# Batch 4 of eight scores its keys on small tiles of TensorE, and a new set of ranks orders all the work

## The chip, the core and the metric

One core of a Trainium2 chip runs the kernel. Its engines work side by side: TensorE multiplies matrices (PE; its weight loads are PEld), VectorE (DVE) and ScalarE (ACT) work on elements, GpSimd (POOL) and SyncE (SP) mostly issue transfers (DMA). The metric is the time of one execution in microseconds (us), as a median of several runs; lower is better.

## The reference

Two attentions follow each other, then two dense layers. The inputs are float32: `q`, `k`, `v` of 8 batches, 8 heads, 576 tokens and 64 values per head, and `p`, 32 landmark tokens per head.

```python
p_packed = sm_attn(p, k, v)           # 32 landmarks look at 576 keys
out = sm_attn(q, p_packed, p_packed)  # 576 queries look at the 32 packed landmarks
x = out.transpose(0, 2, 1, 3).reshape(B * S, H * D)      # 4608 x 512
h = x @ w_in                                             # 512 -> 2048
g = where(h >= 1, h, where(h <= -1, 0, (h + 1)**2 / 4))  # smelu
return g @ w_out                                         # 2048 -> 512
```

`sm_attn` is softmax attention with scale 1/8. The output is 4608 x 512 float32.

## The kernel before

All the work is cut into some 1,500 steps, batch by batch. One batch goes through these stages, each named by its tile and line:

- `k` and `q` are loaded as bf16 by POOL (L352) and turned so that the head's 64 values lie on partitions: in batches 0 and 1 by TensorE (L471), from batch 2 on by a transposing transfer that SP issues (`crossed`, L500, tiles `kT`, `qT`).
- Scores of the landmarks against the keys. There are two forms. In `scores` (L528) the keys are the weights and the landmarks stream through: 24 matmuls of 128 x 64 into `sp`, keys on partitions, then two exponentials on ACT (L533, tile `ex`). In `turned_scores` (L557) the landmarks are the weights, in tiles of 64 rows by 32 columns, and the keys stream: 16 matmuls of 288 columns into two `s1` tiles, landmarks on partitions; ACT takes two exponentials (L564, tile `exn`), each of which also sums its rows into `ks`. There the exponentials lie the wrong way round for the next product, so `untwisted` (L581) turns `exn` back with a transposing transfer on SP into `exT`. `TURN` (L220) is the first batch that takes the second form.
- The packed landmarks `pk` (L619, 24 matmuls): exponentials times values. The values are first regrouped on DVE (L602, tile `vv`, one buffer). In the first form 12 matmuls more, of two columns each (`key_sums`, L634), give the softmax sums; in the second form they are in `ks` already, and DVE makes `rs` from them in two instructions (L666, L667) and not one (L669).
- `ppT` (copies of `pk`), scores of the queries `s2` (L700), exponentials `eT`, sums by a matmul (`sm`, L728), logarithm and exponential for the reciprocal (`ln`, `rc`), the weights of the second attention `A` on DVE (L742); `mp` (L686) is the packed landmarks times `w_in`, copied to `M`.
- The hidden layer `h` (L814, 16 tiles a batch, 4 matmuls each; it needs both halves of `A`), then the smelu in three steps: `x` on ACT (L820), `t` on ACT or DVE (L830, L828), `hT` on DVE (L835).
- The output `o` (L889, 16 matmuls of 512 columns per block of 128 tokens, 36 blocks), a copy `ob`, and two stores by SP (L908).

What stands in which order on each engine is settled while the program is built, in `Plan.run`. Each step has a rank from a table (`AT`, `HID`, `OUT`, `L1`), the engines it may run on with assumed costs, what it depends on and the buffers it takes; a list scheduler with models of the engines, of the load queue and of SP's transfers then picks the ready step of the lowest rank, and the instructions are emitted in that order. On the chip every engine works through its list strictly in order and waits on semaphores, so a step whose input is late holds up all that stands behind it on its engine. `o` matmuls are the material with which the planner fills TensorE while a chain on other engines runs.

Buffers matter for the transfers: one for `k`, one for `v`, one for `vv`, two each for `q`, `kT`, `qT`; three tiles `w` of PSUM are shared by all stages but the output. The load of a batch's `k` waits for the transposing transfer of the batch before to have landed, that of `v` for both `vv` copies of the batch before. All loads stand in one queue on POOL, all transposing transfers and nearly all stores on SP.

Of the kernel before, what the change touches and what calls it, by code (L numbers as in the profile page):

```python
# [183 lines left out]
def kernel(  # L184
# [32 lines left out]
    MB0 = {("k", 0, 4): 0.75, ("v", 0, 0): 1.35, ("q", 0, 0): 0.5}  # L217
    MB1 = {("w_in", 0, 0): 0.7, ("w_in", 0, 1): 0.7}
    FIRST = 2
    TURN = 5  # L220
    PAIRED = 2
    MERGED = 2
    SPLIT, AHALF, WPARTS, MPARTS, QLATE, ORDER3, ORDER = 2, 1, 1, 0, 1, 0, 2
    Q0 = [range(0, 8, 2), range(1, 5, 2), range(5, 9, 2)]
    LOADS = "k0 v0 q0 win0 win1 wout0 k1 win2 win3 wout1 v1 wout2 q1 wout3 v2 q2 p k2"
    LENT = [1, 3, 4]
    L1 = 15.967
    AT = [dict(kT=148.161, qT=275.48, sc=149.063, pk=-49.085, s2=-3.905, sm=-182.602, M=178.569, **{"M+": -129.863}),
          dict(kT=-39.644, qT=-48.123, sc=-66.351, pk=124.743, s2=170.079, sm=-187.478, M=-105.149, **{"M+": 146.812}),
          dict(kT=115.732, qT=51.477, sc=130.42, pk=237.931, s2=-181.084, sm=-29.758, M=169.369, **{"M+": -44.412}),  # L230
          dict(kT=29.446, qT=-25.092, sc=52.472, pk=243.839, s2=179.754, sm=-32.11, M=115.586, **{"M+": -71.343}),
          dict(kT=38.536, qT=86.402, sc=153.04, pk=258.796, s2=-13.152, sm=-43.327, M=-95.344, **{"M+": 110.184}),
          dict(kT=1.864, qT=113.754, sc=282.551, pk=400.409, s2=-26.009, sm=-92.874, M=125.845, **{"M+": 0.958}),
          dict(kT=126.633, qT=239.492, sc=-4.526, pk=382.024, s2=-90.437, sm=32.434, M=177.14, **{"M+": -62.453}),
          dict(kT=27.261, qT=148.76, sc=40.741, pk=216.362, s2=-45.985, sm=130.271, M=1.019, **{"M+": -201.613})]
    HID = [(27.4, 1.3921), (-10.054, 2.601), (22.49, 3.9747), (126.895, 4.8485), (231.121, 9.6612), (-18.141, 4.6461), (3.622, 15.8949), (451.41, 5.8147)]
    OUT = [[(235.954, -183.0), (268.544, -106.533), (35.947, 20.528), (122.624, -48.891)],
# [7 lines left out]

    V, A_, G_ = nc.vector, nc.scalar, nc.gpsimd
    nc.scalar.preload_act_table_set("natural_log_exp_and_others")
# [203 lines left out]
    def attention(b, at, fine):  # L451
# [63 lines left out]
        def scores(i, pairs):  # L515
            n, h0, last = len(pairs), G * pairs[0], (G * pairs[-1] + G) * E - 1

            def mm(e):
                have["sp", b, i] = sp = wide([P, 4 * X * G, n * NP], f32, "sp")
                kT = have["kT", b].rearrange("p h e t -> p (h e t)")  # L520
                for c in range(E):
                    for g in range(G):
                        for k, a in enumerate(pairs):

                            j = (G * a + g) * E + c
                            w = TP if j == last else P
                            o = sp[:w].rearrange("p (c x g) (a n) -> p c x g a n", x=X, g=G, a=n)[:, c, :, g, k]
                            nc.tensor.matmul(o, kT[:, j * TP:j * TP + w], pT[:, b, g, a], start=True, stop=True)  # L528

            def ex(e):  # L530
                if i == 0:
                    have["ex", b] = new("ex", [TP, E * X * G, Q * NP], bf16)
                nc.scalar.activation(have["ex", b][:, :, NP * pairs[0]:NP * (pairs[-1] + 1)],  # L533
                                     have["sp", b, i][:TP, :E * X * G], AF.Exp, scale=scale)

            r = at["sc"] + 0.25 * n * i
            t = plan.add(r, {"PE": (0.03 + 0.18 * n, 0.2 + 0.18 * n, mm)}, ready["k", h0] + pT_of[b],
                         ["w", "ex"] if i == 0 else ["w"])
            x = plan.add(r + 0.01, {"ACT": (0.1 + 0.32 * n, 0.16 + 0.32 * n, ex)}, [t], behind=exs[-1:])
            exs.append(x)  # L540
            plan.release("w", [x])
            return t

        exs = []
        if b == 0:
            pads.append(plan.add(-27, {"DVE": (0.8, 0.8, lambda e: [V.memset(exn[..., TP:], 0.0), V.memset(
                pT[:, 2:TURN].rearrange("p b g a x n -> p (b g a x n)"), 0.0)])},
                                 [consts], behind=ready["k", 4]))

        def turned_scores():  # L550
            def mm(e):
                for g in range(G):
                    have["s1", b, g] = s1 = wide([P, X, FW], f32, "s1")
                    for a in range(Q):
                        for x in range(X):
                            r = slice(x * D, (x + 1) * D)
                            nc.tensor.matmul(s1[a * NP:(a + 1) * NP, x, :HALF], pT[r, b, g, a, x],  # L557
                                             have["kT", b][r, G * a + g].rearrange("p e t -> p (e t)"),
                                             start=True, stop=True)

            def ex(e, g):
                if g == 0:
                    have["ks", b] = new("ks", [P, G], f32)
                nc.scalar.activation(exn[:, g, :, :, :TP],  # L564
                                     have["s1", b, g][:, :, :HALF].rearrange("p x (e t) -> p x e t", e=E),
                                     AF.Exp, scale=scale, accum_out=have["ks", b][:, g:g + 1])

            t = plan.add(at["sc"], {"PE": (0.28, 0.43, mm)}, ready["k", 0] + pT_of[b], ["w"] * G, mode="s")
            before = None
            for g in range(G):  # L570
                ready[f"ex{g}"] = before = plan.add(
                    at["sc"] + 0.2 * g + 0.01, {"ACT": (0.8, 0.87, lambda e, g=g: ex(e, g))}, [t],
                    ["exn", "ks"] if g == 0 else [], behind=[before])
                plan.release("w", [before])
            return t
# [11 lines left out]

        turned_k = b >= TURN
        plan.release("kT", [turned_scores()] if turned_k else [scores(i, ps) for i, ps in enumerate([[0], [1], [2], [3]] if b == 0 else [[0, 1], [2, 3]])])
# [323 lines left out]
    for b in range(B):  # L913
        if b == 2:
            landmarks(2, B, L1, [landed["p"], identity])
        attention(b, AT[b], b == 0)
        for fi in range(KF):
            hidden(b, fi, HID[b][0] + HID[b][1] * fi)
        plan.release("M", h_of[b])
        plan.release("A", h_of[b])  # L920
        first = 0 if b % 2 == 0 else 4
        for j, (start, span) in enumerate(OUT[b]):
            widths = (256, 128, 128) if (b, first + j) == (B - 1, 8) else (d_model,)
# [54 lines left out]
```

## Time and profile before

| | before |
|---|---|
| median of 3 runs | 243.35 us (242.96 to 243.61) |
| profiled execution, its own time | 242.94 us |
| its span, first to last instruction | 241.1 us |
| PE busy | 233.3 us (97%) |
| ACT busy | 192.7 us (80%) |
| DVE busy | 177.6 us (74%) |
| POOL busy | 31.4 us (13%) |
| granted TensorE clock | 1.00 in nearly every stretch |

The profile counts an engine as busy while an instruction is on it. The matmuls of PE overlap in the pipeline, so one of 512 columns is shown with some 379 ns, while the next starts 216 ns after it; what a matmul costs is the distance of the starts, and that is how its rows are read here. The views used are the page with its chain of waits, the busy time by stretches, the instructions in order of time of single engines, the groups by form, and the answers on one line of the program, which tell who waited and how long a transfer took from issue to landing.

### The profile page before, as it was taken

What the parts mean: (1) busy time and instruction counts of PE and PEld (TensorE: products, weight loads), DVE (VectorE), ACT (ScalarE), POOL (GpSimd) and SP (SyncE); (2) the same over time, 40 slices, a digit from 0 to 9 for tenths busy, and PEclk for the clock granted to TensorE, in tenths of its full rate; (3) what the DMA queues carried; (4) which work ended last, traced back from release to release, by engine and by line L of the source; (5) the groups of instructions that cost most, each with busy time, mean ns of one, the idle gap of its engine ahead of it and who ended that gap; (6) DMA issues with size and microseconds to landing.
All of it is one profiled execution on the core that took longest, in us unless ns stands there. A gap on an engine that the chain in (4) does not pass through costs nothing.

```text
span 241.1 us, 5370 instructions
## 1 busy us (share of the span) xinstructions
PE 233.3 (97%) x2117; PEld 133.9 (56%) x2154; DVE 177.6 (74%) x311; ACT 192.7 (80%) x342; POOL 31.4 (13%) x47
## 2 busy tenths in 40 slices
PE   8999999999999999999999999999999999999995
PEld 2646555466554665466645564465546644565454
DVE  4549997678967998789936898689999955899000
ACT  3779996988969985999776988999789988888111
POOL 8462006200220040030030003000000000000000
PEclk9999999999999999999999999999999999999999
DMA  7999999996999999999999999999930301202233
GB/s 158 196 206 207 206 205 205 197 241 132 125 198 149 234 164 251 152 221 221 194 165 246 233 141 147 161 141 226 191 94 4 85 5 44 71 21 65 65 87 90
DMA packets 64138, 37.03 MB, mean 154 GB/s; under 512 B 36720, under 2 KB 59632, under 8 KB 64112
## 3 DMA queue, kind: packets, MB, share of 16 engines
q0 software_dynamic: 24336, 18.25, 52.6%
q1 hardware_dynamic: 38960, 17.87, 36.7%
q10 hardware_dynamic: 816, 0.56, 0.8%
q8 instruction: 17, 0.28, 0.5%
q14 instruction: 9, 0.07, 0.1%
HBM read 37.22 MB, written 9.44 MB: 194 GB/s over the span
## 4 chain that ended last, share of the span: by engine, by line
PE 81%; DVE 6%; DMA 5%; ACT 4%; POOL 2%; issue 2%; POOLq 0%; ACTq 0%
PE o L889 48%; PE h L814 21%; DMA w_in_sb<-in_moe_w_in_dram 5%; DVE hT L835 4%; PE mp L686 3%; PE pk L619 2%; PE sm L728 1%; DVE t L828 1%; ACT x L820 1%; PE sp L528 1%; PE s L700 1%; ACT t L830 1%; POOL q L352 1%; ACT M L271 1%; PE o L942 1%
## 5 line engine op out<-in xcount | busy, mean ns | idle before, releaser
L889 PE MATMUL o<-w_out_sb,hT 128*128 128x512 bf16 (+2 forms) x574 | 140.9, 367 | 1.9 <-issue 0.6
L835 DVE SCALAR_TENSOR_TENSOR hT<-t 128x576 bf16<-128x576 f32 (+1 forms) x130 | 93.7, 746 | 4.3 <-ACT t L830 2.3
L820 ACT ACTIVATE x<-h 128x576 f32<-128x576 f32 (+1 forms) x130 | 78.6, 651 | 9.1 <-PE h L814 8.5
L889 PEld LDWEIGHTS <-hT 128*128 128x128 bf16 x608 | 55.8, 98 | 49.8 <-issue 6.1
L814 PE MATMUL h<-A,M 128*128 128x288 bf16 x512 | 78.5, 286 | 0.6 <-ACT M L271 0.3
L814 PEld LDWEIGHTS <-M 128*128 128x128 bf16 x512 | 49.9, 98 | 27.6 <-issue 1.1
L830 ACT ACTIVATE t<-x 128x576 f32<-128x576 f32 (+1 forms) x57 | 39.4, 693 | 0.6
L828 DVE TENSOR_SCALAR t<-x 128x576 f32<-128x576 f32 (+1 forms) x73 | 33.3, 456 | 7.1 <-ACT x L820 6.7
L271 ACT COPY ob<-o 128x512 f32<-128x512 f32 (+2 forms) x22 | 12.0, 552 | 17.0 <-PE o L889 16.9
L742 DVE SCALAR_TENSOR_TENSOR A<-eT,rs,rc 128x576 bf16<-128x576 bf16 (+1 forms) x18 | 12.8, 748 | 11.5 <-ACT rc L737 11.5
L271 ACT CAST M<-mp 128x1024 bf16<-128x1024 f32 (+1 forms) x20 | 19.1, 992 | 2.7 <-PE mp L686 2.7
L352 POOL DMA_DIRECT2D k<-in_k_dram x8 | 6.7, 843 | 87.8 <-DMA kT<-k 68.4
L271 DVE CAST M<-mp 128x1024 bf16<-128x1024 f32 (+1 forms) x13 | 15.3, 1180 | 3.1 <-PE mp L686 3.1
L271 DVE COPY ob<-o 128x512 f32<-128x512 f32 x16 | 10.8, 688 | 6.9 <-PE o L889 6.9
L723 ACT ACTIVATE eT<-s,rs 128x576 bf16<-128x576 f32 x16 | 11.1, 742 | 2.5 <-PE s L700 2.5
L942 PE MATMUL o<-zeros 128*128 128x512 bf16 (+1 forms) x35 | 10.5, 431 | 1.3 <-DVE zeros L307 1.2
L732 ACT ACTIVATE ln<-sm 128x576 f32<-128x576 f32 x16 | 10.3, 652 | 1.2 <-PE sm L728 0.7
L686 PE MATMUL mp<-w_in_sb,ppT 64*32 64x512 bf16 x256 | 10.9, 380 | 0.2
L271 ACT CAST ppT<-pk 64x128 bf16<-64x128 f32 x24 | 6.2, 260 | 5.7 <-PE pk L634 4.0
L737 ACT ACTIVATE rc<-ln 128x576 f32<-128x576 f32 (+1 forms) x18 | 10.4, 625 | 0.1
L352 POOL DMA_DIRECT2D v<-in_v_dram x8 | 6.2, 779 | 21.9 <-PE pk L624 15.2
L533 ACT ACTIVATE ex<-sp 96x768 bf16<-96x768 f32 (+1 forms) x12 | 8.1, 709 | 0.5 <-PE sp L528 0.4
(59 smaller groups left out, 116.7 us busy)
## 6 DMA issues: line engine op xcount, KB each, us to landing
v<-in_v_dram POOLq DMA_DIRECT2D x8, 576.0 KB, 11.6
out_dram<-ob SPq DMA_DIRECT2D x23, 192.0 KB, 4.5
k<-in_k_dram POOLq DMA_DIRECT2D x7, 576.0 KB, 8.7
q<-in_q_dram POOLq DMA_DIRECT2D x7, 576.0 KB, 12.8
out_dram<-ob SPq DMA_DIRECT2D x24, 128.0 KB, 2.9
w_out_sb<-in_moe_w_out_dram POOLq DMA_DIRECT2D x4, 512.0 KB, 19.7
w_in_sb<-in_moe_w_in_dram POOLq DMA_DIRECT2D x3, 512.0 KB, 15.2
out_dram<-ob SPq DMA_DIRECT2D x23, 64.0 KB, 4.5
```

What stands on the lines that cost most here:

```text
L271: i = (nc.vector.tensor_copy if e == "DVE" else nc.scalar.copy)(to, of)
L352: G_.dma_start(tokens(nm, b)[:, heads(hs)], rows_of(nm, b, hs))
L686: m = nc.tensor.matmul(have["mp", b, f][a * NP:(a + 1) * NP, g], have["ppT", b][r, g, a], w_in_sb[r, a, f * FW:(f + 1) * FW], start=True, ...
L723: nc.scalar.activation(have["eT", b, g], have["s2", b, g][:, :, :HALF], AF.Exp, scale=rs_of[b][:, g, 1:])
L742: V.scalar_tensor_tensor(have["A", b][:, g, xs], have["eT", b, g][:, xs], rs_of[b][:, g, :1], have["rc", b, g][:, xs], ALU.mult, ALU.mult)
L814: nc.tensor.matmul(have["h", b, fi][:, hf, :HALF], have["M", b][:, g, fi * P:(fi + 1) * P], have["A", b][:, g, hf], start=(g == 0), stop=( ...
L820: nc.scalar.activation(have["x", b, fi][:, hs[0]:hs[-1] + 1], have["h", b, fi][:, hs[0]:hs[-1] + 1, :HALF], AF.Prelu, bias=-1.0, alpha=0.5)
L828: V.tensor_scalar(t, x, 1.0, 0.0, ALU.add, ALU.max)
L830: nc.scalar.activation(t, x, AF.Relu, bias=1.0)
L835: V.scalar_tensor_tensor(dst, t, 1.0, t, ALU.min, ALU.mult)
L889: nc.tensor.matmul(have["o", key][:, :w], hT[:, fi, i * P:(i + 1) * P], w_out_sb[:, fi, cols], start=(fi == 0), stop=(fi == KF - 1))
L942: nc.tensor.matmul(o[:, :w], zeros[:, :P], zeros[:, :w], start=True, stop=True)
```

## The change

`TURN` goes from 5 to 4, so batch 4 takes the second form (`turned_scores` and `untwisted`) in place of the first. All numbers of `L1`, `AT`, `HID` and `OUT` are new, so the planner orders all steps anew. No other line differs. Two lines of the table stand for all of it.

```diff
-    TURN = 5
+    TURN = 4
...
-    L1 = 15.967
-    AT = [dict(kT=148.161, qT=275.48, sc=149.063, pk=-49.085, s2=-3.905, sm=-182.602, M=178.569, **{"M+": -129.863}),
...
+    L1 = 24.006
+    AT = [dict(kT=-40.556, qT=-2.912, sc=90.446, pk=28.864, s2=-33.904, sm=-3.662, M=340.906, **{"M+": -180.41}),
```

With it the pad that is zeroed at the start (L546, `pT` of batches 2 to TURN - 1) shrinks from 768 to 512 elements.

What moves, at two places. First SP in the stretch of batch 4's packed landmarks: the turned keys `kT` and queries `qT` of batch 5 (L500), the stores of finished blocks (L908), and the exponentials that are turned back (L581). Before, with nothing to turn back for batch 4; the L581 at the end is batch 5's:

```order
L908 DMA out_0_dram<-ob_1796 96x512
L500 DMA_TRANSPOSE kT_1884<-k_1767 128x24x96
L500 DMA_TRANSPOSE qT_1985<-q_1547 128x24x96
L908 DMA out_0_dram<-ob_2043 64x512 x2
L908 DMA out_0_dram<-ob_2115 96x512
L908 DMA out_0_dram<-ob_2115 32x512
L908 DMA out_0_dram<-ob_2128 32x512
L908 DMA out_0_dram<-ob_2128 96x512
L908 DMA out_0_dram<-ob_2209 64x512 x2
L908 DMA out_0_dram<-ob_2266 64x512 x2
L581 DMA_TRANSPOSE ex_2336<-exn_81 128x12x128
```

The same place on SP now; the L581 here is batch 4's:

```order
L908 DMA out_0_dram<-ob_1735 32x512
L908 DMA out_0_dram<-ob_1801 64x512 x2
L581 DMA_TRANSPOSE ex_1938<-exn_81 128x12x128
L908 DMA out_0_dram<-ob_1985 96x512
L908 DMA out_0_dram<-ob_1985 32x512
L500 DMA_TRANSPOSE kT_2012<-k_1712 128x24x96
L500 DMA_TRANSPOSE qT_2034<-q_1518 128x24x96
L908 DMA out_0_dram<-ob_2037 64x512 x2
```

The transfer that turns batch 4's exponentials back, and the store of one block, now stand ahead of batch 5's `kT` and `qT`.

Second DVE around the weights `A` of batch 2 (L742). The two L602 rows are the regrouping of batch 3's values, which needs the load of batch 3's `v`. Before:

```order
L271 CAST ppT_1214<-pk_1216 64x128 x2
L669 RECIPROCAL rs_1215<-pk_1216 128x4
L271 CAST M_1284<-mp_1285 128x2x512
L271 COPY ob_1307<-o_1000 128x512
L742 SCALAR_TENSOR_TENSOR A_1353<-eT_1295,rs_1215,rc_1321 128x576
L742 SCALAR_TENSOR_TENSOR A_1353<-eT_1301,rs_1215,rc_1351 128x576
L271 CAST M_1284<-mp_1342 128x2x512
L602 COPY vv_1384<-v_1212 96x4x6x64 x2
L835 SCALAR_TENSOR_TENSOR hT_80<-t_1393 128x576
```

The same place on DVE now:

```order
L271 CAST ppT_1219<-pk_1221 64x128 x2
L669 RECIPROCAL rs_1220<-pk_1221 128x4
L271 CAST M_1289<-mp_1290 128x2x512
L602 COPY vv_1313<-v_1163 96x4x6x64 x2
L742 SCALAR_TENSOR_TENSOR A_1364<-eT_1300,rs_1220,rc_1332 128x576
L742 SCALAR_TENSOR_TENSOR A_1364<-eT_1307,rs_1220,rc_1362 128x576
L271 CAST M_1289<-mp_1353 128x2x512
L271 COPY ob_1390<-o_1305 128x512
L835 SCALAR_TENSOR_TENSOR hT_80<-t_1394 128x576
```

The two copies of batch 3's values moved from behind batch 2's `A` to ahead of it.

## Rows read from the trace of the kernel before

**Rows 1.** The page: busy us, share of the span, count of instructions.

```profile
PE 233.3 (97%) x2117; PEld 133.9 (56%) x2154; DVE 177.6 (74%) x311; ACT 192.7 (80%) x342; POOL 31.4 (13%) x47
```

**Rows 2.** The page: the chain that ended last, by engine, share of the span.

```profile
PE 81%; DVE 6%; DMA 5%; ACT 4%; POOL 2%; issue 2%; POOLq 0%; ACTq 0%
```

**Rows 3.** The chain in order of time: start, us, what; two late pieces.

```profile
218.98 0.49 PE h L814 x4
219.47 7.12 PE o L889 x33
```

**Rows 4.** Busy time by stretch: PE, PEld, DVE, ACT, POOL, clock, DMA share, GB/s.

```profile
0.00:10.00 10.00, 8.41 (x71) 4.28 (x73) 5.28 (x20) 5.40 (x11) 7.35 (x15) 1.00 0.94 172
...
110.00:120.00 10.00, 9.90 (x92) 6.40 (x92) 9.82 (x19) 8.71 (x16) 0.00 (x0) 1.00 1.29 203
```

**Rows 5.** PE in order of time: batch 3's first hidden tile, batch 4's scores, sums.

```profile
102.35 0.65 PE L814 MATMUL h<-A,M 128*128 128x288 bf16 x4
...
106.16 0.53 PE L528 MATMUL sp<-pT,kT 128*128 128x64 bf16 x12
106.52 1.07 PE L889 MATMUL o<-w_out_sb,hT 128*128 128x512 bf16 x4
...
117.30 0.44 PE L634 MATMUL pk<-ones,ex 96*128 96x2 bf16 x12
117.61 4.04 PE L889 MATMUL o<-w_out_sb,hT 128*128 128x512 bf16 x17
```

**Rows 6.** PE in order of time: batch 5's scores in the second form.

```profile
134.91 1.24 PE L889 MATMUL o<-w_out_sb,hT 128*128 128x512 bf16 x5
136.08 0.44 PE L557 MATMUL s<-kT,pT 64*32 64x288 bf16 x16
136.45 0.39 PE L889 MATMUL o<-w_out_sb,hT 128*128 128x512 bf16 x1
```

**Rows 7.** ACT groups by form: count, busy us, mean ns, idle before.

```profile
L533 ACT ACTIVATE ex<-sp 96x768 bf16<-96x768 f32 x8 | 6.2, 820 | 0.1
L564 ACT ACTIVATE exn<-s 128x576 bf16<-128x576 f32 x6 | 3.8, 644 | 0.5 <-PE s L557 0.5
L564 ACT ACTIVATION_READ_ACCUMULATOR exn<-s 128x1 f32 x6 | 1.2, 198 | 0.0
```

**Rows 8.** SP in order of time: start, us on SP, what is issued.

```profile
113.69 6.14 SPq L500 DMA_TRANSPOSE kT<-k  x1
...
138.28 1.30 SPq L581 DMA_TRANSPOSE ex<-exn  x1
...
149.34 1.68 SPq L581 DMA_TRANSPOSE ex<-exn  x1
```

**Rows 9.** Line 581, its three transfers: us from issue to landing.

```profile
DMA to landing us min/median/max: 4.4/5.6/14.1
```

**Rows 10.** Line 500 from 113 to 114 us: batch 5's `kT`.

```profile
DMA to landing us min/median/max: 8.3/8.3/8.3
```

**Rows 11.** Line 352 from 106.9 to 107.2 us: the load of batch 6's `q`.

```profile
L352 POOL DMA_DIRECT2D q<-in_q_dram x1: 772/772/772, 106.8 to 106.8; - x1
...
DMA to landing us min/median/max: 13.3/13.3/13.3
```

**Rows 12.** DVE in order of time: batch 2's `A`, batch 3's regrouped values.

```profile
75.17 1.55 DVE L742 SCALAR_TENSOR_TENSOR A<-eT,rs,rc 128x576 bf16<-128x576 bf16 x2 [1.29 <-ACT rc L737]
...
78.42 1.02 DVE L602 COPY vv<-v 96x1536 bf16<-96x1536 bf16 x2 [0.56 <-DMA v<-in_v_dram]
```

**Rows 13.** PE in order of time: batch 2's first hidden tile.

```profile
76.96 0.65 PE L814 MATMUL h<-A,M 128*128 128x288 bf16 x4
```

**Rows 14.** POOL in order of time: loads of batch 3's `q` and `v`.

```profile
64.41 0.77 POOL L352 DMA_DIRECT2D q<-in_q_dram  x1
68.73 0.77 POOL L352 DMA_DIRECT2D v<-in_v_dram  x1 [3.55 <-DVE vv L602]
```

**Rows 15.** Line 352 from 64.5 to 65.1 us: the load of batch 3's `q`.

```profile
DMA to landing us min/median/max: 8.2/8.2/8.2
```

More of the change, by code (lines that the diff above doesn't have):

```diff
@@ L226 @@
     LENT = [1, 3, 4]
-    L1 = 15.967
-    AT = [dict(kT=148.161, qT=275.48, sc=149.063, pk=-49.085, s2=-3.905, sm=-182.602, M=178.569, **{"M+": -129.863}),
[L229 to L235, printed above, removed]
@@ L236 @@
-    HID = [(27.4, 1.3921), (-10.054, 2.601), (22.49, 3.9747), (126.895, 4.8485), (231.121, 9.6612), (-18.141, 4.6461), (3.622, 15.8949), (451.41, 5.8147)]
-    OUT = [[(235.954, -183.0), (268.544, -106.533), (35.947, 20.528), (122.624, -48.891)],
[7 rows of a table removed]
+    L1 = 24.006
+    AT = [dict(kT=-40.556, qT=-2.912, sc=90.446, pk=28.864, s2=-33.904, sm=-3.662, M=340.906, **{"M+": -180.41}),
+          dict(kT=-43.72, qT=1.836, sc=-0.038, pk=31.835, s2=156.584, sm=81.675, M=23.068, **{"M+": 117.307}),
+          dict(kT=409.892, qT=18.256, sc=-85.757, pk=13.961, s2=102.318, sm=-96.638, M=80.744, **{"M+": 100.138}),
+          dict(kT=16.476, qT=-13.225, sc=-74.324, pk=16.65, s2=-0.231, sm=-91.19, M=238.622, **{"M+": -174.524}),
+          dict(kT=-92.914, qT=394.922, sc=127.068, pk=77.016, s2=-1.879, sm=-81.232, M=9.357, **{"M+": -47.465}),
+          dict(kT=236.026, qT=289.414, sc=258.533, pk=8.919, s2=61.139, sm=13.02, M=2.931, **{"M+": 49.515}),
+          dict(kT=446.079, qT=-90.885, sc=-99.845, pk=334.341, s2=62.656, sm=-266.482, M=-0.476, **{"M+": -150.224}),
+          dict(kT=106.934, qT=4.407, sc=339.865, pk=24.137, s2=-80.103, sm=81.912, M=96.817, **{"M+": -116.888})]
@@ L246 @@
+    HID = [(0.443, 1.4101), (-10.544, 2.3596), (-113.458, 5.7876), (115.962, 1.3103), (191.855, 8.3497), (32.692, 1.4181), (-61.597, 1.8225), (395.63, 8.5607)]
+    OUT = [[(360.324, 29.52), (356.37, -148.384), (350.737, 34.476), (112.645, -47.685)],
[7 rows of a table added]
     V, A_, G_ = nc.vector, nc.scalar, nc.gpsimd
```

14 rows, old and new, of the table OUT are left out of this document.

## The prediction

> **What bounds the kernel now.** I read the page first. PE is busy 97% of the span, ACT 80%, DVE 74% [rows 1], and the chain that ended last is PE for 81% of its length [rows 2]. The reader should see that no other engine comes near, and then ask whether a busy PE is also a PE at its pace, since a matmul that waits a little between others still shows as busy. The late piece of the chain answers that: 33 matmuls of 512 columns in 7.12 us, 0.216 us each, with nothing between; a hidden tile of four takes 0.49 us there [rows 3]. By stretches of 10 us, PE shows 8.41 in the first, where the chain of loads, transposes and exponentials of batch 0 has nothing to overlap with, and 9.90 in the stretch of batch 4's packed landmarks, at a clock of 1.00 [rows 4]. So from about 45 us on PE is the bound, and work taken from PE shortens the kernel by its own length, as long as no wait takes its place. What happens before that is set by batch 0's chain, and there the new order of PE, ACT and DVE is almost the old one: I count nothing there.
>
> **What PE saves in batch 4.** Removed are two groups of 12 score matmuls: the first starts at 106.16, the next work at 106.52, 0.36 us a group, 0.72 together; and the 12 sums of two columns, from 117.30 to 117.61, 0.31 us [rows 5]. That is 1.03 us. Added are 16 matmuls in the second form. Batch 5's show the price, with what it costs to go in and out of it: the five matmuls ahead start at 134.91 and end their pace at 134.91 + 5 x 0.216 = 135.99, the small ones start at 136.08, the next work at 136.45 [rows 6]. So 0.09 + 0.37 = 0.46 us. PE gains 1.03 - 0.46 = 0.57 us.
>
> That 0.46 holds a rule which speaks against the change. The rows show 0.09 us of nothing ahead of the small tiles. The Trainium skill (TensorEngine Tiling (Array Packing), Key Properties) says that a change of the tiling mode drains TensorE, and the trace agrees with this 0.09. Without a drain the saving would be 0.66 us; with one it is the 0.57 above.
>
> **What the other engines get.** ACT gives up two exponentials of 820 ns (1.64 us) and gets two of 644 with a read of 198 each (1.68 us) [rows 7]. DVE gets one instruction more, on two values a partition, which I put at the length of that read. Both lie beside PE, which has the longer sum; without that cover they would cost 0.2 us together. The smaller pad at the start saves DVE at most 0.2 us and nothing waits for it. I take 0 for all three.
>
> **The transposing transfer that comes in.** `pk` of batch 4 now waits for it. When is it issued, and when is it wanted? In the new order on PE 9 hidden tiles and 17 output matmuls stand from batch 3's first hidden tile to the scores of batch 4. That tile starts at 102.35 [rows 5], about 0.4 us sooner in the new order, two output matmuls fewer being ahead of it. The scores then start at 101.9 + 9 x 0.49 + 17 x 0.216 + 0.1 = 110.1. For batch 5 the transfer was issued 2.2 us after the scores began (138.28 against 136.08) [rows 6, 8]; so here at 112.3. From the scores to `pk` stand the scores, 7 hidden tiles and 32 output matmuls: 0.4 + 3.43 + 6.9 = 10.7 us. `pk` is due at 120.8, and the transfer has 8.5 us.
>
> The trace has three such transfers: 4.4, 5.6 and 14.1 us to landing [rows 9]. So the added wait costs from 0 to 14.1 - 8.5 = 5.6 us. The nearest row is batch 5's `kT`, in the very stretch: issued at 113.69, landed after 8.3 us, at 122.0 [rows 8, 10], and it turns half as much again (24 x 96 columns against 12 x 128). It ran into the load of batch 6's `q`, under way from 106.8 to 120.1 [rows 11]. The new transfer is smaller, is issued 1.4 us sooner and stands ahead of `kT`, so I put its landing at 119 to 121 and the wait at 0, with 0.5 us at hand. Queued behind it on SP are a block's store and batch 5's `kT` and `qT`, and on POOL the load of batch 6's `k`, which waits for that `kT`. It moves them by some 2 us: its own issue, 1.3 to 1.7 us [rows 8], and the store's. `kT` would land near 124; batch 5's scores are at 136 [rows 6]. That delay is hidden.
>
> The Trainium skill (Advanced Engine Details and Errata, X-Bar Transpose (TRN2)) says that transposing transfers are as fast as ordinary ones. The rows don't bear that out where loads are under way: one size of transfer took 4.4 and 14.1 us. By the rule the wait is nothing and the sum is the same; by the slowest row it is the first rival below.
>
> **What the new order moves elsewhere.** PE has the same matmuls in the same stages, other output matmuls between them; with PE at its pace this costs nothing unless a step comes late. One place stands out. DVE now has the two copies of batch 3's values ahead of batch 2's `A`, and all else on DVE is behind them; PE's hidden tiles of batch 2 wait for `A`. Before, these copies started at 78.42, having waited 0.56 us for the load, and `A` had long been done (75.17 to 76.72) [rows 12]; the first hidden tile started at 76.96 [rows 13]. In the new order four more output matmuls stand ahead of that tile, so it is due at 76.96 + 0.86 = 77.8, and its second half of `A` at 78.05. After the landing come 1.02 us of copies and 1.55 of `A`; so the load must land by 75.5. Each us later costs one. The load went out at 68.73, after 3.55 us of waiting for the second copy of batch 2's values [rows 14]. In the new order both those copies stand together, sooner, and at most the whole wait goes: landing from 78.4 - 3.55 = 74.9 to 78.4. It can't pass the load of `q` ahead, which landed at 64.41 + 8.2 = 72.6 [rows 14, 15]. So the cost is 0 to 2.9 us. I take 0, since most of the wait goes; this is my least sure term.
>
> **The sum.** -0.57 + 0 + 0 = -0.57 us against the profiled execution: 242.94 us, of which 241.1 is the span, to 242.4. It lay 0.41 us below the median of the runs shown, so the median goes from 243.35 to 242.8; I say 242.75.
>
> **The rivals.**
> 1. The transposing transfer is late and `pk` waits. For it: 14.1 us of batch 6's transfer, issued at 149.34 beside two loads. Against: the margin of 0.5 us and the later stages, which have the same transfer with room. If loads hold it to 122 or 123, the wait is 1.2 to 2.2 us and the time 243.9 to 245; if to 14.1 us, 248.4. It decides from 1.3 us past 120.8, where it eats the saving and more.
> 2. The load of batch 3's values is late, DVE stands in front of `A` and PE in front of the hidden tiles. For it: the new order on DVE, and that the load landed only at 78.4. Against: it is issued sooner. At 78.4 the loss is 2.9 us and the time 245.7; at 77 it is 1.5 and 244.3. From 76.1 on the saving is gone. This is the one that ends slower, at that one place.
> 3. The saving happens on PE and is taken back by small waits of the new order: an output matmul that comes closer to its `hT`, or a transfer at its due time. PE's saving is 0.57 us, so some 0.3 to 0.6 us of such waits leave 243.0 to 243.4, no change.
> 4. The new order also takes away waits that PE still has. The stretch shown has 0.10 us of 10 without PE [rows 4], over the 195 us from 45 us on 2 us, of which the drains stay. I give this rival a third, 0.7 us, beside the 0.57: 242.1.
>
> **How the numbers follow.** About 0.3%, 0.73 us, is what a measurement of this kernel tells from no change; faster means below 242.6, slower above 244.1. My forecast as worked out (242.4 to 243.0) has 0.42, and a third of it lies below 242.6. Rival 1 has 0.13, rival 2 0.20, rival 3 0.10, rival 4 0.15, all of the last faster. Of rivals 1 and 2 two thirds end slower, the rest between. Faster: 0.14 + 0.15, and a little more for the early chain, in all 0.32. Slower: 0.22, and 0.03 for waits that I haven't seen. Same: 0.43. The range for 8 in 10 goes from 241.8 (rival 4 with a gain in the early chain) to 245.0 (rival 2 at a landing of 77.7); the forecast's own is 242.3 to 243.1.
>
> **What would show it.** In the profile of the changed kernel: 16 matmuls of L557 in batch 4 near 110, 24 of L528 and 12 of L634 fewer, and PE's busy time down by about half a us. The landing of batch 4's L581 before 120.8, and no idle time of PE's weight loads ahead of `pk`; a wait there on the transfer is rival 1. On DVE the L602 copies near 76 and `A` right behind; DVE idle on the load of `v` and PE idle on DVE's `A` ahead of L814 near 78 is rival 2. If PE's span falls by 0.6 and the time doesn't, it is rival 3. The prediction is wrong if PE's waits after 45 us change by more than 0.7 us in all.

## The result and the profile after

The changed kernel takes 244.34 us (median of 22 runs, 242.28 to 247.06), the kernel before 243.12 us beside it (22 runs, 242.13 to 244.31). The ratio is 1.0039, with a 95% interval of 1.002 to 1.0057: slower by 0.4%, where I had forecast 242.75 us. All ratios in this document leave out executions that are more than 1.5% above the fastest of the same kernel, here three of the 22 (246.19, 246.62 and 247.06 us); the medians, which hold them, stand 1.22 us or 0.5% apart. The times also scatter over 4.8 us, where those of before scatter over 2.2.

The profiled execution took 244.31 us, its span 242.5 us against 241.1. First the page of the changed kernel: busy us, share of the span and count, as in [rows 1], and the chain by engine, as in [rows 2].

```profile
PE 235.2 (97%) x2134; PEld 132.5 (55%) x2134; DVE 178.9 (74%) x310; ACT 191.8 (79%) x346; POOL 30.3 (13%) x47
...
PE 72%; DMA 15%; DVE 6%; ACT 3%; issue 1%; POOL 1%; POOLq 0%
```

PE's busy time can't be compared with that of before: the change takes matmuls away, yet the page shows more of them, because the page of before holds 574 of the program's 608 output matmuls and this one all 608. The chain is what changed. PE carries 72% of it and not 81%, DMA 15% and not 5%. Nine of the 15 are loads of `k` and `v` in the first 25 us. The other 6 are two pieces, in order of time (start, us, what):

```profile
112.77 9.45 DMA ex<-exn
...
141.69 5.74 DMA ex<-exn
```

These are the transposing transfers of batches 4 and 5, from issue to landing: 122.22 and 147.43. PE in order of time at the two `pk` that wait for them, with the idle time that the profile puts ahead of a row in brackets:

```profile
117.17 4.70 PE L889 MATMUL o<-w_out_sb,hT 128*128 128x512 bf16 x21
122.35 0.86 PE L619 MATMUL pk<-ex,vv 96*128 96x64 bf16 x24 [0.48 <-DMA ex<-exn]
...
146.21 0.81 PE L889 MATMUL o<-w_out_sb,hT 128*128 128x512 bf16 x3
147.48 0.88 PE L619 MATMUL pk<-ex,vv 96*128 96x64 bf16 x24 [0.46 <-DMA ex<-exn]
```

By pace, `pk` of batch 4 was due at 117.17 + 21 x 0.2158 = 121.70 and came 0.65 us late; that of batch 5 at 146.21 + 3 x 0.2158 = 146.86, 0.62 us late. (The brackets show less, since the profile models the end of a matmul, and that end covers a part of the wait.) The stretches show it as well: PE's busy time from 120 to 130 us and from 140 to 150, columns as in [rows 4], of the changed kernel

```profile
120.00:130.00 10.00, 9.52 (x108) 4.38 (x107) 5.61 (x9) 6.63 (x13) 2.31 (x3) 1.00 1.09 190
140.00:150.00 10.00, 9.54 (x100) 5.64 (x99) 8.75 (x18) 8.22 (x16) 0.00 (x0) 1.00 1.04 146
```

and of the kernel before:

```profile
120.00:130.00 10.00, 9.95 (x89) 4.33 (x89) 5.33 (x9) 7.28 (x10) 2.32 (x3) 1.00 1.08 191
140.00:150.00 10.00, 9.89 (x91) 5.78 (x92) 9.48 (x19) 9.49 (x21) 1.29 (x2) 1.00 1.09 153
```

The rows that answer to [rows 12, 13] show DVE with the copies of batch 3's values ahead of `A`, and then PE's first hidden tile of batch 2:

```profile
75.57 1.03 DVE L602 COPY vv<-v 96x1536 bf16<-96x1536 bf16 x2 [1.03 <-DMA v<-in_v_dram]
76.51 1.54 DVE L742 SCALAR_TENSOR_TENSOR A<-eT,rs,rc 128x576 bf16<-128x576 bf16 x2
```
```profile
78.22 0.65 PE L814 MATMUL h<-A,M 128*128 128x288 bf16 x4
```

The load landed at 75.47, and in this execution PE waited for nothing there.

Five executions of the changed kernel were profiled in all, the first and four more (`e5_changed_again`, `p1` to `p3` below). Late means late against PE's pace, worked out as above; the last column is the span less the three waits.

| time, us | span | late at `h` of batch 2 | late at `pk` 4 | late at `pk` 5 | span less these |
|---|---|---|---|---|---|
| 243.35 | 241.6 | 0 | 0.18 | 0.63 | 240.8 |
| 243.79 | 242.0 | 0 | 0.28 | 0.59 | 241.1 |
| 244.31 | 242.5 | 0 | 0.65 | 0.62 | 241.2 |
| 244.90 | 243.1 | 1.50 | 0 | 0.69 | 240.9 |
| 246.36 | 243.6 | 0 | 1.53 | 0.69 | 241.4 |

Spans that differ by 2.0 us lie within 0.6 us of each other once the three waits are taken off. The scatter of these five spans is theirs. That of the times isn't quite: the longest lies 2.8 us over its span and the other four 1.8. In that execution a transfer of 16 KB on the queue that carries instructions started at 245.3 us, behind the last instruction; the other four have none there. Of the 22 executions five lie 2.4 us or more over their spans, while no execution of the kernel before whose span is on record lies more than 1.94 over. What such a transfer costs was not tested. And three of the five longest of the 22 (245.40, 245.58 and 247.06 us) had a granted clock of 0.991 to 0.993, all others 0.998 or more, so their length need not be waits.

### The profile page after: what moved, and what is told of

The parts are those of the page before. It is cut to its first block, busy times and chain, and to the rows that moved or that the text cites. A ratio compares the mean times of both kernels' runs of the same rounds, so it can differ in the third digit from the quotient of the medians.

```text
span 242.5 us, 5383 instructions
## 1 busy us (share of the span) xinstructions
PE 235.2 (97%) x2134; PEld 132.5 (55%) x2134; DVE 178.9 (74%) x310; ACT 191.8 (79%) x346; POOL 30.3 (13%) x47
## 4 chain that ended last, share of the span: by engine, by line
PE 72%; DMA 15%; DVE 6%; ACT 3%; issue 1%; POOL 1%; POOLq 0%
PE o L889 44%; PE h L814 18%; DMA ex<-exn 6%; DMA k<-in_k_dram 6%; DVE hT L835 4%; DMA v<-in_v_dram 3%; PE mp L686 3%; PE pk L619 2%; DVE t L828 1%; PE sm L728 1%; ACT x L820 1%; PE s L700 1%; PE tp L471 1%; ACT t L830 1%; PE sp L528 1%
## 5 line engine op out<-in xcount | busy, mean ns | idle before, releaser
L889 PE MATMUL o<-w_out_sb,hT 128*128 128x512 bf16 (+2 forms) x608 | 147.2, 368 | 0.3 <-DVE hT L835 0.2
L830 ACT ACTIVATE t<-x 128x576 f32<-128x576 f32 (+1 forms) x58 | 40.1, 694 | 0.7
L271 ACT COPY ob<-o 128x512 f32<-128x512 f32 (+2 forms) x21 | 11.4, 545 | 19.2 <-PE o L889 19.2
L271 DVE CAST M<-mp 128x1024 bf16<-128x1024 f32 (+1 forms) x15 | 17.8, 1185 | 4.0 <-PE mp L686 3.8
L271 DVE COPY ob<-o 128x512 f32<-128x512 f32 x17 | 11.6, 688 | 11.9 <-PE o L889 11.9
L271 ACT CAST M<-mp 128x1024 bf16<-128x1024 f32 (+1 forms) x18 | 17.1, 988 | 1.3 <-PE mp L686 1.2
L352 POOL DMA_DIRECT2D k<-in_k_dram x8 | 6.2, 778 | 93.4 <-DMA kT<-k 73.1
L742 DVE SCALAR_TENSOR_TENSOR A<-eT,rs,rc 128x576 bf16<-128x576 bf16 (+1 forms) x18 | 12.7, 746 | 5.7 <-ACT rc L737 5.6
L271 ACT CAST ppT<-pk 64x128 bf16<-64x128 f32 x26 | 6.8, 260 | 5.3 <-PE pk L619 2.0
L602 DVE COPY vv<-v 96x1536 bf16<-96x1536 bf16 x12 | 6.2, 549 | 2.5 <-PE pk L619 1.5
```

The lines of the kernel that those rows point to most:

```text
L271: i = (nc.vector.tensor_copy if e == "DVE" else nc.scalar.copy)(to, of)
L352: G_.dma_start(tokens(nm, b)[:, heads(hs)], rows_of(nm, b, hs))
L742: V.scalar_tensor_tensor(have["A", b][:, g, xs], have["eT", b, g][:, xs], rs_of[b][:, g, :1], have["rc", b, g][:, xs], ALU.mult, ALU.mult)
L830: nc.scalar.activation(t, x, AF.Relu, bias=1.0)
L889: nc.tensor.matmul(have["o", key][:, :w], hT[:, fi, i * P:(i + 1) * P], w_out_sb[:, fi, cols], start=(fi == 0), stop=(fi == KF - 1))
```

## The experiments

Ratios are to the kernel before, run on the same chip beside each kernel, with 95% intervals; each timed kernel has 12 runs, `e3` and `e4` have 6.

**Take both waits away.** `e1_pk45_no_wait`: 0.999 (0.9965 to 1.0016).

```diff
+                if b in (4, 5):
+                    ex = w_in_sb[:TP, 0, :G * X * E * P].rearrange("t (g x e a n) -> t e x g a n", g=G, x=X, e=E, a=Q)
```

> In batches 4 and 5 `pk` multiplies values that stand ready in SBUF (the weights of `w_in`) instead of the exponentials turned back; the transposing transfers still run, so the results of these two batches' attention are other ones. Theory A (the change loses where TensorE waits for the transposing transfers of batches 4 and 5: 0.65 us ahead of and in `pk` of batch 4 and 0.63 us at batch 5, 1.27 us by their rows): both stretches run at pace, the profiled span falls by about 1.3 us against the changed kernel (242.5 to about 241.2), and the median comes to 0.995 to 0.999 of the kernel before. Rival B (many small waits of the new ranks, none at `pk`, cost it): at most 0.3 us comes back, 1.002 to 1.005 of the kernel before. Rival C (the wait at `pk` 4 and 5 moves to the next wait, at `h` or at batch 6's keys): the rows at `pk` are gone and the time stands within 0.3 us of the changed kernel's.

(Lines are numbered two higher in this kernel.) The rows of PE at batch 4 show no gap: 21 output matmuls from 119.18 end at 123.71, where `pk` starts.

```profile
119.18 4.70 PE L891 MATMUL o<-w_out_sb,hT 128*128 128x512 bf16 x21
123.71 0.86 PE L621 MATMUL pk<-w_in_sb,vv 96*128 96x64 bf16 x24
```

The median fell as theory A has it; rivals B and C are out. But the profiled execution (245.02 us, the longest of the 12) had a wait that I had seen nowhere yet: batch 3's `v` landed at 77.88, and PE stood 1.49 us at batch 2's first hidden tile. So the span, 243.2, didn't fall to the 241.2 that I expected. That is my rival 2, in one execution and not in another.

**Take one load out of the way.** `e2_q6_behind_k6`: 1.0036 (1.001 to 1.0062).

```diff
+    order.remove(landed["q", 6, 0][0])
+    order.insert(order.index(landed["k", 6, 0][0]) + 1, landed["q", 6, 0][0])
```

> POOL's load of batch 6's q is issued behind batch 6's k load instead of at 104.9 us, some 8 us ahead of the transposing transfer of batch 4 (issued 112.8, landed 122.2, with the q load's landing at 121.3); nothing else is changed. Theory A (a transposing transfer lands only about when the loads issued ahead of it have drained): the transfer of batch 4 lands at 117 to 119.5, 5 to 7 us after its issue, `pk` of batch 4 does not wait, and the time falls by 0.4 to 0.7 us against the changed kernel, unless batch 6's q, now late, holds up its own turning. Rival B (the transfer is slow by itself or by SP's own queue): it takes 9 us or more again, landing at 121.5 to 122.5, and the time stays within 0.2 us of the changed kernel's. In both, the transfer of batch 5 (issued 141.7) keeps its 5.7 us unless the q load now falls into it.

Line 581 from 112 to 113 us, issued at 112.29:

```profile
DMA to landing us min/median/max: 5.7/5.7/5.7
```

5.7 us in place of 9.4, landing at 117.97, and `pk` of batch 4 on time (21 output matmuls from 116.70 end at 121.23):

```profile
116.70 4.70 PE L889 MATMUL o<-w_out_sb,hT 128*128 128x512 bf16 x21
121.23 0.86 PE L619 MATMUL pk<-ex,vv 96*128 96x64 bf16 x24
```

For the transfer theory A holds and rival B falls. `pk` of batch 5 was still 0.77 us late, and the median shows no gain, which theory A had wrong. The profiled execution (243.34 us) is the fastest of its 12, so it doesn't show what held the others up.

**One half of the change at a time.** `e3_new_ranks_turn5`: 1.0646 (1.0594 to 1.0698). `e4_old_ranks_turn4`: 1.0377 (1.0335 to 1.0419).

```diff
-    TURN = 4
+    TURN = 5
```
```diff
-    TURN = 5
+    TURN = 4
```

> The new ranks alone: batch 4 is scored and turned as before (exponentials by TensorE's own form, no transposing transfer), in the changed kernel's order of ranks as the planner lays it for that form. Theory A (the transposing transfer of batch 4 and what it pushes, batch 5's, is the loss): no wait at `pk` of batch 4, that of batch 5 at most 0.3 us; 0.57 us of TensorE work comes back, 1.3 us of waiting goes: 0.996 to 1.000 of the kernel before. Rival B (the new ranks lose by themselves): 1.002 to 1.008 of the kernel before, with the lost time spread or at a new place in batches 0 to 3.

> The new form of batch 4 alone, in the ranks of the kernel before. Theory A (the form's transfer is what is late): issued about 112 to 114 and landing near 121 to 123, with `pk` of batch 4 due by the old ranks near 120 to 121, so TensorE waits 1 to 2.5 us there; 1.002 to 1.010 of the kernel before. Rival B (the new ranks lose, the form gains): TensorE's 0.57 us shows in the time, 0.996 to 0.999 of the kernel before, with under 0.3 us of waiting at `pk` of batch 4.

Both miss by far: these kernels take much longer than either expectation. The chain by engine of the first and of the second:

```profile
PE 62%; DVE 16%; ACT 12%; DMA 4%; issue 3%; POOL 1%; ACTq 0%; POOLq 0%; DVEq 0%
```
```profile
PE 65%; DVE 13%; ACT 10%; DMA 7%; issue 2%; SPq 1%; POOL 1%; ACTq 0%; POOLq 0%; DVEq 0%
```

PE's share falls to 62 and 65%, and DVE and ACT take it. A table of ranks that was settled for one form lays out another program for the other form, so this pair says nothing on the shares of form and ranks. One reading is of use: in `e4` the transfer of batch 4 was issued at 109.44, 3.3 us sooner than in the changed kernel, and landed at 125.05, 0.2 us behind batch 6's `q` load.

**The changed kernel again, and DVE's old order.** `e5_changed_again`: 1.0035 (1.0001 to 1.007). `e6_vv3_behind_A`: 1.0026 (1.0 to 1.0052).

```diff
...
+    for t in vv_of[3]:
+        order.remove(t)
+    at = [i for i, t in enumerate(order) if t.engine == "DVE" and i > order.index(A_of[2][-1])][0] + 1
+    order[at:at] = vv_of[3]
```

> The changed kernel once more, beside the three edits of it. Theory V (in some executions batch 3's `v` load lands so late that DVE's copies of it, now ahead of batch 2's `A`, hold up `h` of batch 2, as in the first experiment's profile: landing 77.88, TensorE idle 0.85 and 0.31 us for `A`; in the changed kernel's first profile the landing was 75.47 and nothing waited): its times scatter over 3 us or more again, the ratio lies at 1.002 to 1.006, and a second profile shows the landing anywhere from 75 to 78.5, with TensorE's wait about the landing less 75.9. Without theory V the landing is 75.5 to 76 again.

> One edit of the changed kernel, on DVE alone: batch 3's two copies of `v` stand behind batch 2's two `A` and the `M` that follows, as in the kernel before. Theory V: `h` of batch 2 waits no more, whatever the landing; the slow end of the scatter goes (highest time 1 us or more below that of the changed kernel on this chip) and the median falls by 0.4 to 0.9 us (0.2 to 0.4%), while the 1.27 us at `pk` of batches 4 and 5 stays. Rival W (the waits at `pk` are the whole loss): the time stays within 0.25 us of the changed kernel's.

`e5` has the landing at 76.20 and no wait for `A`. In `e6` no `A` waits for `v`, but its profile has the price elsewhere. POOL in order of time, changed kernel and then `e6`:

```profile
103.11 0.77 POOL L352 DMA_DIRECT2D k<-in_k_dram  x1 [17.37 <-DMA kT<-k]
103.87 0.77 POOL L352 DMA_DIRECT2D v<-in_v_dram  x1
104.90 0.77 POOL L352 DMA_DIRECT2D q<-in_q_dram  x1 [0.26 <-issue]
```
```profile
105.00 0.77 POOL L352 DMA_DIRECT2D k<-in_k_dram  x1 [19.32 <-DMA kT<-k]
105.76 0.77 POOL L352 DMA_DIRECT2D v<-in_v_dram  x1
106.79 0.77 POOL L352 DMA_DIRECT2D q<-in_q_dram  x1 [0.26 <-issue]
```

The loads that go with batch 4's transfer start 1.9 us later, that transfer lands at 124.15, and `pk` of batch 4 waits 2.5 us:

```profile
124.28 0.86 PE L619 MATMUL pk<-ex,vv 96*128 96x64 bf16 x24 [2.32 <-DMA ex<-exn]
```

The longest executions didn't go, against theory V: the two longest executions of `e6` took 248.57 and 249.25 us (at a granted clock of 0.993), those of `e5` 246.73 at most. The edit trades one late transfer for another, and doesn't tell theory V from W.

**Make `pk` due later.** `e7_o_ahead_of_pk`: 1.0054 (1.0027 to 1.0081). `e8_both`, with `e6`'s edit as well: 1.0053 (1.0022 to 1.0083).

```diff
...
+    for b, n in ((4, 4), (5, 4)):
+        first, last = order.index(pk_of[b]), order.index(h_of[b][0])
+        moved = [t for t in order[first:last] if t in o_of.values()]
+        to = {pk_of[b]: moved[:n], **dict(zip(moved, [[t] for t in moved[n:]]))}
...
```

> One edit of the changed kernel, on TensorE alone: four of the `o` matmuls (0.86 us) that stand between `pk` and the first `h` of batches 4 and 5 are issued ahead of `pk`, the others move up, so that each `pk` is due 0.86 us later. Theory A (waits of 0.65 and 0.63 us for the transposing transfers): both waits go, nothing new waits in `s2`, `sm` or the first `h`, since those follow `pk` as they did; the time falls by 0.9 to 1.3 us (0.4 to 0.5%). Rival C: the chain from `pk` to the first `h` needs the same 8 us from the transfer's landing, there are now four `o` fewer ahead of that `h`, and 0.3 to 0.65 us of wait at each comes back there: the time falls by 0.5 us or less.

> Both edits together, with all of the new form kept. Theory V and A together: 1.3 to 2.1 us under the changed kernel, 0.995 to 0.998 of the kernel before (what is left of the form is its 0.57 us of TensorE work, against some 0.4 us of waiting in the first 35 us). If the waits only move, it stays at 1.000 to 1.003.

Theory A missed: the waits at `pk` went, but others came and the time didn't fall. They stand mostly not where rival C had put them, ahead of the first `h`, but at output matmuls. PE in order of time behind `pk` of batch 5 in `e7`:

```profile
150.36 0.70 PE L889 MATMUL o<-w_out_sb,hT 128*128 128x512 bf16 x2 [0.16 <-issue]
151.34 0.82 PE L889 MATMUL o<-w_out_sb,hT 128*128 128x512 bf16 x3 [0.28 <-DVE hT L835]
152.53 0.81 PE L889 MATMUL o<-w_out_sb,hT 128*128 128x512 bf16 x3 [0.36 <-DVE ob L271]
```

By pace these are some 0.5 us for an `hT` and as much for the copy that frees PSUM: the output matmuls that were drawn forward came too early for both.

**Mend the transfer of batch 5, then both.** `e9_exn5_together`: 1.0045 (1.0017 to 1.0074). `e10_q6_exn5`, which adds `e2`'s edit: 1.0006 (0.998 to 1.0032); the same kernel once more as `e14_repairs_again`: 0.9993 (0.9972 to 1.0014).

```diff
...
+    order.remove(ex_of[5, 1])
+    order.insert(order.index(ex_of[5, 0]) + 1, ex_of[5, 1])
```

> One edit of the changed kernel, on ACT alone: the second exponential of batch 5 stands right behind the first, not behind an `x` that waits 0.55 us for its `h`. Theory X (batch 5's transfer is late because the new ranks score its keys 1.1 us nearer to `pk` and set that `x` between the two exponentials): the transfer is issued about 1.2 us earlier, lands 1 to 1.2 us earlier (5.5 to 6 us after its issue), the 0.6 us of wait at `pk` of batch 5 goes, and the time falls by 0.4 to 0.6 us. Rival L (its landing is set by the loads, the last of which lands at 142.6): it lands at 147 as before and the time stays within 0.15 us of the changed kernel's (1.003 to 1.004 of the kernel before).

> Both repairs of the transposing transfers, nothing left out: batch 6's q load behind batch 6's k load (so that the transfer of batch 4 has one load fewer ahead of it) and batch 5's two exponentials together. Theory A and X: the transfer of batch 4 lands at 117.5 to 119, that of batch 5 a microsecond earlier, no wait at either `pk`; 1.0 to 1.3 us under the changed kernel, 0.998 to 1.001 of the kernel before in the median, with batch 3's `v` left as the source of scatter. If these waits are not what is lost: 1.002 to 1.005.

> The two repairs alone once more, beside it, for a second estimate of what they give: theory A and X 0.998 to 1.002 of the kernel before, as the first time (1.0006); if that run was luck, 1.003 or more, as the changed kernel.

ACT in order of time at batch 5's exponentials, kernel before, changed kernel and then `e9`:

```profile
136.90 0.63 ACT L564 ACTIVATE exn<-s 128x576 bf16<-128x576 f32 x1
137.43 0.19 ACT L564 ACTIVATION_READ_ACCUMULATOR exn<-s 128x1 f32 x1
137.52 0.64 ACT L564 ACTIVATE exn<-s 128x576 bf16<-128x576 f32 x1
```
```profile
139.11 0.65 ACT L564 ACTIVATE exn<-s 128x576 bf16<-128x576 f32 x1
139.64 0.20 ACT L564 ACTIVATION_READ_ACCUMULATOR exn<-s 128x1 f32 x1
140.39 0.65 ACT L820 ACTIVATE x<-h 128x576 f32<-128x576 f32 x1 [0.55 <-PE h L814]
140.93 0.65 ACT L564 ACTIVATE exn<-s 128x576 bf16<-128x576 f32 x1
```
```profile
137.97 0.65 ACT L564 ACTIVATE exn<-s 128x576 bf16<-128x576 f32 x1
138.50 0.20 ACT L564 ACTIVATION_READ_ACCUMULATOR exn<-s 128x1 f32 x1
138.59 0.65 ACT L564 ACTIVATE exn<-s 128x576 bf16<-128x576 f32 x1
```

The second exponential starts 0.62 us after the first and not 1.82 us. The transfer of `e9` was issued at 139.37 and landed at 143.29, and `pk` of batch 5, at 145.72, was on time: theory X. But the transfer took 3.9 us where I expected 5.5 to 6, so more than its earlier issue helped, and no run shows what. The median of `e9` didn't move, against theory X. Its profiled execution (242.69 us) had no wait at `pk` of batch 4 either (landing at 120.53), so it isn't a typical one. It took both edits to move the median. In `e10` (and in all three profiles of that kernel) both `pk` start at pace, the second with 0.08 us to spare (landing at 146.22):

```profile
117.26 4.70 PE L889 MATMUL o<-w_out_sb,hT 128*128 128x512 bf16 x21
121.79 0.86 PE L619 MATMUL pk<-ex,vv 96*128 96x64 bf16 x24
...
145.65 0.81 PE L889 MATMUL o<-w_out_sb,hT 128*128 128x512 bf16 x3
146.30 0.86 PE L619 MATMUL pk<-ex,vv 96*128 96x64 bf16 x24
```

Nothing is left out of the computation there, and the loss is gone twice. The interval of the first time (up to 1.0032) overlaps that of the changed kernel (from 1.002), that of the second (up to 1.0014) doesn't.

**Batch 4's `q` load later.** `e11_q4_q6_exn5`, with both repairs: 1.0006 (0.9984 to 1.0028). `e12_q4_no_wait`, with the edit of `e1` in their place: 1.0002 (0.9976 to 1.0028).

```diff
+    order.remove(landed["q", 4, 0][0])
+    order.insert(order.index(landed["k", 4, 0][0]) + 1, landed["q", 4, 0][0])
```

> The same two repairs and a third: POOL's load of batch 4's q stands behind batch 4's k load (issued about 83 us in place of 67.1), so that it no longer shares the queues with batch 3's `v`. Theory V (batch 3's `v` is the third late transfer): `v` lands 1 to 2 us earlier (73.5 to 74.5) and nothing waits at batch 2's `A`; batch 4's q, late now, has until its turning and batch 4's second scores at 124 us; 0.996 to 0.999 of the kernel before and scatter no wider than that of the kernel before. Rival: pushing that load into batch 5's set of loads delays the transfer of batch 4 or batch 4's keys again: 1.000 to 1.005.

> The bound: batches 4 and 5 multiply values that stand ready (as in the first experiment; their attention is another one), and batch 4's q is loaded behind batch 4's k, so that none of the three late transfers can hold up TensorE. Theory A, V and X: 0.994 to 0.998 of the kernel before, below the first experiment's 0.999. If batch 3's `v` is of no weight: 0.998 to 1.000, as the first experiment.

Batch 3's `v` landed at 76.66 and 76.24, no sooner, where I had expected 73.5 to 74.5: the load behind it was not what held it. Neither beats the two repairs. But `v` was as late as ever in them, so they are no bound, and what a sooner `v` would give the median stays open.

**Four executions more**, for the table above; `p4` is `e10`'s kernel (243.86 us, both `pk` at pace).

> The changed kernel, one more execution with its profile, read for which wait goes with its time. Theory A: its time follows the two waits for transposing transfers (by the three executions profiled so far, the transfer of batch 4 lands 0.9 to 1.2 us behind batch 6's q load): one at 244 us or less has waits of 0.3 to 0.7 us at `pk` of batch 4, one at 245.5 us or more has 1.5 us or more there or at batch 5. Theory V: the slow ones wait at batch 2's `A` instead, with batch 3's `v` landing past 77. If a slow execution shows neither, the scatter comes from elsewhere (the first 20 us, where the first loads land).

> The same, another execution: the same readings of the waits at `pk` of batches 4 and 5, at batch 2's `A` and in the first 20 us against its time.

> The same, another execution, to tell whether time and those waits go together over several.

> The changed kernel with both repairs (batch 6's q load behind batch 6's k load, batch 5's exponentials together), one more execution: theory A and X hold if neither `pk` waits over 0.2 us in it too, with batch 4's transfer landing 1 to 2 us behind batch 5's `v`.

The longest is theory A's and the second longest theory V's (the shortest waited 0.18 us at `pk` of batch 4, less than the 0.3 that theory A has). PE in order of time, the one of 246.36 us and the one of 244.90 us:

```profile
117.30 4.70 PE L889 MATMUL o<-w_out_sb,hT 128*128 128x512 bf16 x21
123.36 0.86 PE L619 MATMUL pk<-ex,vv 96*128 96x64 bf16 x24 [1.36 <-DMA ex<-exn]
```
```profile
79.38 0.42 PE L814 MATMUL h<-A,M 128*128 128x288 bf16 x2 [0.86 <-DVE A L742]
80.10 0.41 PE L814 MATMUL h<-A,M 128*128 128x288 bf16 x2 [0.30 <-DVE A L742]
```

In the latter `v` landed at 77.48 and `A` started at 78.51. The waits there, by pace 1.03 us at the first two matmuls and 0.47 at the next two, also gave batch 4's transfer the time it needed.

**A wait in front.** `e13_o_ahead_of_h13`, with both repairs: 0.9982 (0.9958 to 1.0007).

```diff
...
+    for t in [t for t in order[order.index(h_of[0][-3]):] if t in o_of.values()][2:4]:
+        order.remove(t)
+        order.insert(order.index(h_of[0][-3]), t)
```

> The changed kernel with both repairs of the transfers (batch 6's q load behind batch 6's k load, batch 5's exponentials together) and one edit in batch 0: two `o` matmuls that stood behind its 14th hidden tile stand ahead of it. In all nine profiles of kernels with the new ranks read so far TensorE stands 0.35 us there, for ACT's `x` to free PSUM, which the kernel before doesn't. Theory S (small waits of the new order, this one in the front, take back the 0.57 us of the new form): the gap goes, 0.3 us, and the time comes to 0.997 to 1.000 of the kernel before. Rival: ACT sets the pace there, the gap moves to the next hidden tile and the time stays as with the two repairs alone.

The gap of 0.35 us is gone, but the next hidden tile comes 0.25 us late (two output matmuls at 34.19 end by pace at 34.62):

```profile
33.70 0.65 PE L814 MATMUL h<-A,M 128*128 128x288 bf16 x4
34.19 0.59 PE L889 MATMUL o<-w_out_sb,hT 128*128 128x512 bf16 x2
34.87 0.65 PE L814 MATMUL h<-A,M 128*128 128x288 bf16 x4
```

Most of it moved, as the rival has it. This is the lowest ratio of all; its interval still holds 1, so it isn't shown to beat the kernel before.

## Why the prediction was wrong

- **PE's saving: right in kind.** The matmuls went as counted. What stands ahead of batch 4's small tiles: 6 output matmuls from 109.55 end by pace at 110.85, the small tiles start at 110.98, 0.13 us later, where I put 0.09. That agrees with what the Trainium skill (TensorEngine Tiling (Array Packing), Key Properties) says of a drain, but the amount comes from the rows alone.
- **The transposing transfer of batch 4: the step that failed.** I wrote "I put its landing at 119 to 121 and the wait at 0". Issue (112.77 for 112.3) and due time (121.70 for 120.8) were near, with 8.9 us of room; the landing was 122.2, and 121.3 to 123.2 in the other four executions. I had the cause in hand, batch 6's `q` load in [rows 11] and `kT` that "ran into" it, and then argued from size and place in the queue. Neither held: the transfer landed 0.9, 1.0, 0.9, 0.7 and 1.0 us behind that load in the five executions (the first: load issued at 104.90, 16.4 us, landed at 121.28). With this, my own rows give 120.2 + 0.9 = 121.1 for a due time of 120.8. Rival 1 happened, at 0 to 1.5 us, from execution to execution.
- **The transfer of batch 5: a term that I put at nothing.** I priced moved steps in one place and wrote that the rest "costs nothing unless a step comes late". Rival 3 named such a wait ("a transfer at its due time"), but I gave it 0.10 and looked at no row for it. The new ranks put batch 5's scores 8.2 us ahead of `pk` (138.67 to a due time of 146.86), where before it was 9.2 (136.08 to 145.24), and put an `x` between the two exponentials. The transfer went out 3.0 us after the scores and not 2.2, took 5.7 us (the median of [rows 9] is 5.6), and cost 0.6 to 0.7 us in all five executions. This is the steadiest part of the loss.
- **Batch 3's `v`: a spread and not a value.** I put the landing that was needed at 75.5; a landing at 76.20 cost nothing (`e5`), so there was more room than that. It came at 75.1 to 77.5 in five executions, and cost 0 in four and 1.50 us in one. I took it for one unknown value, and chose 0; it differs from execution to execution.
- **The sum.** -0.57 us of work and +0.8 to +2.2 us of waits make +0.2 to +1.7 us; the medians differ by 1.2. That the 244.34 us lie in my range is no merit of the mechanism: the sum had both waits at 0. `e1`, `e10` and `e14` show that without the waits at the two `pk` the loss is gone. Why neither repair alone moved the median (`e2`, `e9`) isn't settled: each leaves the other wait, and their intervals reach 0.6 us to either side, as much as one wait is worth. Nor does the saving stand out in any kernel without those waits. Two small waits that the kernel before doesn't have are candidates, both against the prediction's "I count nothing there" or its "costs nothing": 0.35 us in batch 0, which `e13` moved more than it removed, and an output matmul near 86 us that stood 0.3 to 0.4 us for its `hT` in three of the five executions.
- **The rule on transfers.** The Trainium skill (Advanced Engine Details and Errata, X-Bar Transpose (TRN2)) has transposing transfers as fast as ordinary ones. I set it aside for [rows 9]. In the changed kernel one size again took 3.7 to 12.1 us, but ordinary loads of one size spread as well there (6.2 to 16.4 us), so neither spread tells the two kinds of transfer apart and the rule stays untested here. The sum didn't use it.

## What to carry to other kernels

When a change hangs the busiest engine on one more transfer, ask which loads are already under way when it is issued, and take the landing of the last of them as the earliest landing, or the issue plus the transfer's own time where that is later. Compare every wait of the moved program with its due time, those that only moved closer too. And where a due time and a landing lie within a microsecond, expect a spread of times and not a number.

## What the runs showed of the hardware

With loads under way, batch 4's transposing transfer on SP landed when the loads issued ahead of it had landed, not a fixed time after its own issue:

| kernel | last load ahead, landed | transfer of batch 4 issued | landed |
|---|---|---|---|
| `e4_old_ranks_turn4` | 124.84 (`q`) | 109.44 | 125.05 |
| `e6_vv3_behind_A` | 123.48 (`q`) | 112.86 | 124.15 |
| changed | 121.28 (`q`) | 112.77 | 122.21 |
| `e1_pk45_no_wait` | 120.14 (`q`) | 114.77 | 121.38 |
| `e10_q6_exn5` | 118.70 (`v`) | 112.86 | 120.01 |
| `e2_q6_behind_k6` | 116.47 (`v`) | 112.29 | 117.97 |

It took 5.7 to 15.6 us and lands 0.2 to 1.5 us behind the last load in each. An early issue didn't help: the earliest has the latest landing. Moving one load of 576 KB gave 3.8 us back. `e2` shows that the load delays the transfer; by what mechanism the two share the way, no run shows.

The last load gives only the earliest landing. Batch 5's transfer in the changed kernel was issued 0.9 us before the last load ahead landed (142.58) and took 5.7 us all the same. And a load issued just behind can count too: in the kernel before, batch 6's transfer (the 14.1 us of [rows 9], issued at 149.34, landed at 163.46) came 0.45 us behind a load that was issued at 149.78.
